# Attention batch 0 by query tiles, k in q's layout, zero products in gaps, and six x matrices turned by DMA

## Chip, core and metric

The kernel runs on one core of one Trainium2 chip. The metric is the device time of one execution in microseconds (us); the median of the runs shown is 271.3 us. One core has five engines that work from queues of their own: TensorE (PE in the profile, its weight loads PEld), VectorE (DVE), ScalarE (ACT), GpSimd (POOL) and SyncE (SP). SP here only issues DMAs; POOL issues some too and also computes.

## What is computed

For 8 batches and 12 heads, with 448 rows of 64 numbers: cosine attention, then a highway layer over the 3584 rows that the heads form together.

```python
q_n = q / (norm(q, axis=-1) + 1e-06);  k_n = k / (norm(k, axis=-1) + 1e-06)
scores = q_n @ k_n.T / tau                      # tau = 0.1
attn = softmax(scores);  x = attn @ v           # x: (8*448, 12*64) = (3584, 768)
H = relu(x @ w_h);  T = sigmoid(x @ w_t + b_t)
out = T * H + (1 - T) * x
```

The kernel leaves out the maximum of the softmax and the small constants, and makes the sigmoid from a tanh.

## The kernel before

**Work.** Heads are taken in pairs (p = 0..5 in a batch), and pairs in groups of two (g = 0..2). A batch goes through: loads (`ld_q` L293 on SP, `ld_k` L308 and `ld_v` L323 on POOL with a cast to fp16, tails of 64 rows `ld_kt`, `ld_vt` on SP); squares on ACT and sums on DVE (`norm_q`, `norm_k`, `norm_t`); an inverse root by seven small DVE steps (`newton`); scaling (`scale_q` L434, `scale_k` L495, `scale_kb` L502, nearly all on POOL); turning q and k with TensorE transposes and a DVE copy from PSUM (`turn_q` L446/L451, `turn_k` L460/L465/L471); `scores`; `attend`; and `ffn` for four row tiles.

**Layouts.** q is loaded so that a lane holds seven neighbouring rows (448 = 64 lanes x 7) of one head; two heads fill 128 lanes. The main part of k is 128 lanes x 3 rows of a head, and its last 64 rows come in a load of their own, are scaled apart (`kb`, zeros around them) and turned apart: eight transposes for a group, six of `kp` and two of `kb`.

**Attention** (`scores` L524, `attend` L548). For a pair: six products of 64x128 weights with 448 columns (L531) and one for both tails (L542), each followed by an exponential of 448 columns on ACT (L537, L544); then 3 x (1 + 6) products with 130 or 65 columns (L556, L561) and eight for the last 64 queries (L569); a reciprocal and a division on DVE (L576, L577) that write x. All 448 queries of a pair go at once, so x of a batch is complete only after its sixth pair.

**Highway layer** (`ffn` L583). A batch has three tiles of 128 rows and one that holds the last 64 twice, side by side. A tile's x is turned by six (three in the last tile) TensorE transposes (L600) and a DVE copy (L602); 24 products of 384 columns with w_t and w_h follow (L616; L613 in the last tile), then DVE and ACT work, sums on POOL (L642) and stores on SP (L649, L652).

**Order.** A `Plan` collects 1915 named operations in the program's order. `ORDER` is a list of their numbers, written out by hand or by a program elsewhere: every engine gets its operations in this order and works through them in it. `SLOTS` says which buffer of a ring each tile takes (`B` is the ring of the eight PSUM banks). Operations in `PORT` make a POOL operation wait for the DVE operation before it in `ORDER`. 18 products of zeros (`WARM`, L279) run at the start.

Of the kernel before, what the change touches and what calls it, by code (L numbers as in the profile page):

```python
# [93 lines left out]
""".split()  # L94
)

SLOTS = {
    "qr": "01010101",
    "kr": "0120120",
    "kt": "01010101",  # L100
    "kb": "01010101",
    "kp": "012345012345012345012345012345021435021435120534",
    "vr": "01010101",
    "vt": "01011010",
    "vp": "01010101",
# [96 lines left out]
def kernel(  # L202
# [11 lines left out]
    nc = tc.nc  # L214
# [555 lines left out]
```

## Time and profile before

| | us |
|---|---|
| runs: median (lowest to highest) of 3 | 271.3 (270.35 to 271.45) |
| the profiled execution | 270.06 |
| its span, first to last instruction | 268.3 |
| PE busy in the span | 251.6 (94%) |
| DVE busy | 233.4 (87%) |
| ACT busy | 214.5 (80%) |
| POOL busy | 169.8 (63%) |

The profile is of one execution. Matmuls are pipelined: one is shown from its start to its modelled end, so PE can look busy while it waits. The chain of waits goes back from the last instruction to whatever released each step, and gives every stretch of time to one engine or transfer. The granted clock is the share of TensorE's full clock that the chip gave it.

### The profile page before, as it was taken

Reading aid. Unit: us, or ns where it says so; the run is one execution under the profiler, and the core shown is the slowest. Engines: PE = TensorE matmul, PEld = TensorE weight load, DVE = VectorE, ACT = ScalarE, POOL = GpSimd, SP = SyncE. Lnnn points to the kernel's source line nnn. Section 1 sums busy time; section 2 is a strip of 40 time slices with the busy share of each in tenths; the row PEclk is TensorE's granted clock in tenths of the full one; section 3 lists DMA queues with packets and bytes.
Section 4 is the critical chain, followed back from the end, with each engine's and each line's share of the span. In section 5 each row is a group of like instructions: output and inputs, shape, how many; then the busy total and the mean of one; then the engine's idle time right before and its main releaser. Section 6 shows DMA issues by size and latency. Waiting matters only on the chain.

```text
span 268.3 us, 7687 instructions
## 1 busy us (share of the span) xinstructions
PE 251.6 (94%) x3042; PEld 158.8 (59%) x3042; DVE 233.4 (87%) x523; ACT 214.5 (80%) x421; POOL 169.8 (63%) x212
## 2 busy tenths in 40 slices
PE   8375999999999999999999999999999999999990
PEld 2122566656756576657656685666666675667660
DVE  2987988799999999999989899999998788657993
ACT  3389899999589997999899996999979757883120
POOL 6467878306975679668957397659555686320650
PEclk9755799999999999999999999999999999999998
DMA  7999999999307990496995972990513101052146
GB/s 173 298 290 181 208 270 261 213 255 126 44 18 221 234 182 14 146 257 159 151 142 185 164 107 67 330 135 4 147 23 100 29 15 49 0 147 65 29 135 190
DMA packets 51092, 38.64 MB, mean 144 GB/s; under 512 B 37488, under 2 KB 47856, under 8 KB 51056
## 3 DMA queue, kind: packets, MB, share of 16 engines
q1 hardware_dynamic: 25888, 26.75, 36.2%
q0 software_dynamic: 24896, 11.21, 33.1%
q8 instruction: 24, 0.39, 0.5%
q10 hardware_dynamic: 272, 0.20, 0.2%
q14 instruction: 12, 0.10, 0.1%
HBM read 38.34 MB, written 11.01 MB: 184 GB/s over the span
## 4 chain that ended last, share of the span: by engine, by line
PE 81%; DMA 6%; DVE 4%; ACT 4%; SPq 1%; issue 1%; POOL 1%; ACTq 0%; DVEq 0%
PE B L616 33%; PE B L531 12%; PE B L561 10%; PE B L613 5%; DMA os<-in_k_dram 4%; PE B L556 4%; PE B L600 4%; PE B L446 3%; PE B L542 3%; PE B L569 3%; PE B L460 3%; ACT E L537 3%; DMA out_dram<-os 1%; PE B L465 1%; DVE hm L628 1%
## 5 line engine op out<-in xcount | busy, mean ns | idle before, releaser
L537 ACT ACTIVATE E<-B 128x448 f16<-128x448 f32 x288 | 137.4, 577 | 15.6 <-PE B L531 12.6
L642 POOL TENSOR_TENSOR os<-x,hm 128x384 f32<-128x384 f16 x53 | 47.5, 911 | 50.2 <-DVE hm L637 39.6
L616 PEld LDWEIGHTS <-xT 128*128 128x128 f16 x576 | 51.2, 98 | 34.8 <-issue 7.5
L434 POOL TENSOR_TENSOR qn<-qr,y 128x448 f16<-128x448 f32 x47 | 43.4, 934 | 24.6 <-issue 8.1
L616 PE MATMUL B<-wh,xT 128*128 128x384 f16 x288 | 57.6, 326 | 0.0
L616 PE MATMUL B<-wt,xT 128*128 128x384 f16 x288 | 56.7, 326 | 0.0
L531 PE MATMUL B<-qT,kT 64*128 64x448 f16 x288 | 43.5, 367 | 2.8 <-DVE kT L473 1.5
L561 PE MATMUL B<-vp,E 128*128 128x65 f16 x864 | 44.5, 195 | 0.0
L561 PEld LDWEIGHTS <-E 128*128 128x128 f16 x864 | 39.1, 99 | 2.9
L632 ACT ACTIVATE tt<-z 128x768 f16<-128x768 f32 (+1 forms) x32 | 25.3, 793 | 18.5 <-DVE z L625 14.8
L495 POOL TENSOR_TENSOR kp<-kr,y 128x384 f16<-128x384 f16 x42 | 34.3, 827 | 8.2 <-DVE tt L634 2.6
L628 DVE SCALAR_TENSOR_TENSOR hm<-B,x 128x384 f16<-128x384 f32 x56 | 30.5, 549 | 3.0 <-PE B L616 1.7
L556 PE MATMUL B<-vp,Et 128*128 128x130 f16 x144 | 32.3, 224 | 0.0
L625 DVE TENSOR_TENSOR z<-B,bias 128x384 f32<-128x384 f32 x48 | 25.9, 551 | 6.5 <-PE B L616 5.5
L544 ACT ACTIVATE Et<-B 128x448 f16<-128x448 f32 x48 | 27.9, 597 | 3.1 <-PE B L542 2.8
L577 DVE SCALAR_TENSOR_TENSOR x<-B,rd 128x448 f16<-128x448 f32 x48 | 29.2, 617 | 0.6
L376 DVE TENSOR_REDUCE n<-sq 128x14 f32<-128x896 f32 (+1 forms) x25 | 25.8, 1040 | 1.2 <-ACT sq L368 1.2
L397 DVE TENSOR_REDUCE n<-sq 128x18 f32<-128x1152 f32 (+2 forms) x17 | 21.5, 1269 | 4.2 <-ACT sq L388 3.8
L368 ACT ACTIVATE sq<-qr 128x896 f32<-128x896 f32 (+1 forms) x24 | 23.1, 978 | 1.1 <-DMA qr<-in_q_dram 1.1
L531 PEld LDWEIGHTS <-kT 64*128 64x128 f16 x288 | 10.3, 94 | 20.1 <-issue 12.3
L556 PEld LDWEIGHTS <-Et 128*128 128x128 f16 x144 | 14.1, 98 | 7.9 <-issue 4.7
L542 PE MATMUL B<-qT,kT 128*128 128x448 f16 x48 | 17.4, 371 | 1.1 <-DVE kT L475 1.1
(59 smaller groups left out, 363.3 us busy)
## 6 DMA issues: line engine op xcount, KB each, us to landing
qr<-in_q_dram SPq DMA_DIRECT2D x7, 1344.0 KB, 7.6
out_dram<-os SPq DMA_DIRECT2D x48, 192.0 KB, 3.3
kr<-in_k_dram POOLq DMA_DIRECT2D x7, 576.0 KB, 12.2
vr<-in_v_dram POOLq DMA_DIRECT2D x7, 576.0 KB, 10.3
kt<-in_k_dram SPq DMA_DIRECT2D x16, 96.0 KB, 6.4
vt<-in_v_dram SPq DMA_DIRECT2D x16, 96.0 KB, 7.5
out_dram<-os SPq DMA_DIRECT2D x16, 96.0 KB, 2.9
qr<-in_q_dram SPq DMA_DIRECT2D x3, 448.0 KB, 6.9
```

The costliest lines, as they stand in the source:

```text
L434: ENG[eng].tensor_mul(R("qn", 3 * b + g)[:, :, t, :], R("qr", b)[:, g + 3 * t, :].rearrange("l (j d) -> l j d", d=D), R("y", b)[:, c : c + ...
L495: ENG[eng].tensor_mul(R("kp", 6 * b + p).rearrange("l c t d -> l t c d"), a, kcol(b, p))
L531: nc.tensor.matmul(R("B", ("S", n, c, t))[:, 0:S], lhsT=R("kT", i)[ln, s, 128 * c : 128 * c + 128], rhs=R("qT", i)[ln, s, :], start=True, ...
L537: nc.scalar.activation(R("E", n)[:, at : at + 7, :].rearrange("l j x -> l (j x)"), R("B", ("S", n, c, t))[:, 0:S], AF.Exp)
L544: op("ACT", f"expt {n}", lambda: nc.scalar.activation(R("Et", n).rearrange("l j x -> l (j x)"), R("B", ("St", n))[:, 0:S], AF.Exp), r=[("B ...
L556: nc.tensor.matmul(U[:, 2 * c : 2 * c + 2, :], lhsT=Et[:, 2 * c : 2 * c + 2, :].rearrange("l j x -> l (j x)"), rhs=vp[:, 6:8, 0:65], start ...
L561: nc.tensor.matmul(U[:, 2 * c + t, :], lhsT=E[:, at : at + 2, :].rearrange("l j x -> l (j x)"), rhs=vp[:, 3 * t + m, 0:65], start=False, s ...
L577: op("DVE", f"ev {n}", lambda: nc.vector.scalar_tensor_tensor(out=R("x", b)[:, :, D * p : D * p + D], in0=U_()[:, :, 0:D], scalar=0.0, in1 ...
L616: nc.tensor.matmul(P[:, 0:MH], lhsT=xT[:, cc, :], rhs=w_[:, cc, MH * mh : MH * mh + MH], start=(cc == 0), stop=(cc == CC - 1))
L625: op("DVE", f"za {g} {mh}", lambda at=at, sl=sl: nc.vector.tensor_add(R("z", g)[:, sl], R("B", at)[:, 0:MH], biast[:, :] if tail else bias ...
L628: op("DVE", f"hm {g} {mh}", lambda at=at, sl=sl, mh=mh: nc.vector.scalar_tensor_tensor(out=R("hm", g)[:, sl], in0=R("B", at)[:, 0:MH], sca ...
L642: op(eng, f"out {g} {mh}", lambda sl=sl, mh=mh: ENG[eng].tensor_add(R("os", g)[:, sl], xpart(mh), R("hm", g)[:, sl]), r=[("gg", g), ("x", ...
```

## The change

- **k like q.** k is loaded with q's layout (64 lanes x 7 rows, rows of 896 bytes after the cast), for batch 0 too, where before it came in fp32 on the SP and ACT queues. The tail's load, square, sum, scaling and zeros in `kb` go. `norm`, `scale` and `turn` serve q and k alike: a group of k has seven transposes, one copy of 2 x 384 columns and two small copies (`cpt`) of its last 64 rows; zeros around those are set once.
- **Inverse roots of batch 0** by two ACT operations (`lnexp`: exp(-0.5 ln)) for each group in place of seven DVE steps. ACT loads table set 6 first and set 0 after them (`table2`).
- **Batch 0 by query tiles** (`attend0`): for tile i of 128 queries (the last of 64), all three groups; x of tile i is complete when they are through, and `ffn(0, i)` reads that tile alone.
- **Zero products**: 37 more (`wf`), placed in `ORDER` among the first operations of PE.
- **x of batches 1 to 6** is turned by a transposing DMA on SP (`xd`, 24 of them: 18 of [128, 768] and 6 of [128, 384]), from x straight into xT. Batches 0 and 7 keep transposes and copies.
- **Rings**: kT and qT 3 to 4 buffers, xT 3 to 5.
- **Held loads**: a load of q or of v's tail for batch 1 or later waits for the ACT operation before it in `ORDER`.
- **ORDER and SLOTS** are new (1946 operations).

```diff
-PORT = ("nt", "gt", "gg", "vc", "qn", "kn", "kb", "vt", "out")
+PORT = ("nt", "gt", "gg", "vc", "qn", "kn", "vt", "out")
+        self.held = eng == "SP" and kind in ("ldq", "ldvt") and name.split()[1] != "0"
...
-    WARM = 18
+    WARM, NF = 18, 37
+    XDMA = range(1, B - 1)
+    LG = ((0, 0), (0, 28), (0, 56))
...
+    for i in range(NF):
+        op("PE", f"wf {i}", lambda i=i: nc.tensor.matmul(R("B", ("F", i))[:, :], lhsT=wz[:, 0:128], rhs=wz[:, 128:640],
+                                                         start=True, stop=True), r=[("wz",)], w=[("B", ("F", i))], mode="F")
...
+    def q_src(t, b):
+        return t[b].rearrange("(u s) (l j) d -> s l u (j d)", s=2, j=NJ)
+    def ld_qk(nm, b, gs=range(3)):
+        t, eng = (q, "SP") if nm == "q" else (k, "POOL")
...
+    def lnexp(b, lo, hi, parts):
+        i = (b, lo)
+        op("ACT", f"ln{hi - lo} {b} {lo}", lambda: nc.scalar.activation(
+            R("tu", i)[:, 0, lo:hi], R("n2", b)[:, lo:hi], AF.Ln, bias=eps[:, 0:1]),
...
+        op("ACT", f"ie{hi - lo} {b} {lo}", lambda: nc.scalar.activation(
+            R("y", b)[:, lo:hi], R("tu", i)[:, 0, lo:hi], AF.Exp, scale=-0.5),
...
+        if nm == "k":
+            for t in range(2):
+                ln = slice(64 * t, 64 * t + 64)
+                op("DVE", f"cpt {b} {g} {t}", lambda ln=ln, t=t: nc.vector.tensor_copy(
+                    turned("k", i)[ln, :, 384 + 64 * t : 448 + 64 * t], src()[ln, :, 384:448]),
...
+    def attend0(g, i):
+        q_, k_ = turned_of(g)
+        w = 128 if i < 3 else 64
...
+                    for c in range(NC):
+                        for t in range(2):
+                            ln, at = slice(64 * t, 64 * t + 64), unit(s)[0][t][c] - o - 512 * t
+                            nc.tensor.matmul(R("B", (A, B_)[t])[:, at : at + w], lhsT=k_()[ln, s, 128 * c : 128 * c + 128],
+                                             rhs=q_()[ln, s, 128 * i : 128 * i + w], start=True, stop=True)
...
+            for t, X, m in ((0, A, 512), (1, B_, 384)):
+                op("ACT", f"ex{m} {n}", lambda X=X, m=m, t=t, o=o: nc.scalar.activation(
+                    flat()[:, o + 512 * t : o + 512 * t + m], R("B", X)[:, 0:m], AF.Exp),
...
+        def turn_dma():
+            X = R("x", b)
+            nc.sync.dma_start(R("xT", g)[:, 0:nb, :], X[:, 6, :] if tail else X[:, 2 * i : 2 * i + 2, :].rearrange("l j m -> l (j m)"),
+                              transpose=True)
+        if b in XDMA:
+            op("SP", f"xd{nb} {g}", turn_dma, r=[xk], w=[("xT", g)])
+        else:
...
+                elif o.held:
+                    behind(made[0], act)
```

In the new order PE gets 41 zero products before its first transposes (`tk 0 0`, `tq 0 0`) and 14 in later gaps. The exponentials of query tiles 0 and 1 of all three groups stand ahead of most of tile 2's, and the first products of `ffn` follow them. An `xd` stands in SP's order soon after the last division of its batch; between that division and the first product that reads its xT, PE has other work:

| first tile of a batch | PE operations between |
|---|---|
| batch 1, tile 4 | 4 qk, 2 ff, 1 tk, 2 tq, 2 qkt |
| batch 2, tile 8 | 5 qk, 2 ff, 1 tk, 2 tq, 3 qkt, 3 av |
| batch 3, tile 12 | 4 qk, 2 ff, 2 tk, 2 tq, 2 qkt, 3 av |
| batch 4, tile 16 | 7 qk, 2 ff, 2 tk, 1 tq |
| batch 5, tile 21 | 3 qk, 4 ff, 2 fft, 1 tk, 2 tq |
| batch 6, tile 25 | 5 qk, 4 ff, 2 tk, 3 qkt, 6 av, 2 avt |

(qk is two products of 448 columns, qkt one, ff three of 384, fft six on half the columns, tk and tq seven transposes each, av 1 + 6 products, avt eight.)

More of the change, by code (lines that the diff above doesn't have):

```diff
@@ L121 @@
[L121 to L128 removed]
+    "qT": "01230123012301231023102",
@@ L144, in __init__ @@
         kind = name.split()[0].rstrip("0123456789")
-        self.port = eng in ("DVE", "POOL") and (kind in PORT or kind == "sqq")
+        self.held = eng == "SP" and kind in ("ldq", "ldvt") and name.split()[1] != "0"
+        self.port = eng in ("DVE", "POOL") and (kind in PORT or kind == "sq")
 class Plan:
@@ L220 @@
     NC, NJ = 3, 7
-    WARM = 18
+    WARM, NF = 18, 37
+    XDMA = range(1, B - 1)
+    GROUPS = ((0, 1), (1, 2), (2, 3)), ((0, 1), (1, 3)), ((0, 3),)
+    LG = ((0, 0), (0, 28), (0, 56))
+    SCALE = {("q", 0, 0): ("DVE", "POOL"), ("k", 0, 0): ("DVE", "POOL")}
     tau = float(tau)
@@ L273, with zf @@
                                     (t[0:64, :, 6, D : D + 1], 1.0), (t[64:128, :, 7, D : D + 1], 1.0)]), w=[("zvp",)])
-    for i, t in enumerate(TILES["kb"]):
-        op("DVE", f"zkb {i}", zero("DVE", [(t[0:64, :, 1, :], 0.0), (t[64:128, :, 0, :], 0.0)]), w=[("zkb",)])
-    op("DVE", "zw", zero("DVE", [(wz[:, :], 0.0)]), w=[("wz",)])
+    for i, t in enumerate(TILES["kT"]):
+        op("DVE", f"zkT {i}", zero("DVE", [(t[0:64, :, 448:512], 0.0), (t[64:128, :, 384:448], 0.0)]), w=[("zkT",)])
+    def zf():
+        t = turned("k", 0)
+        zero("DVE", [(t[0:64, :, 448:512], 0.0), (t[64:128, :, 384:448], 0.0)])()
+    op("DVE", "zkf", zf, w=[("x", "f", "z")])
+    op("DVE", "zw", zero("DVE", [(wz[:, :], 0.0), (eps[:, :], 1e-14)]), w=[("wz",), ("eps",)])
     for i in range(WARM):
@@ L344, in ld_b, with col @@
         op("SP", "ldb", fn, w=[("b",)])
[L347 to L366 removed]
+    def col(nm, g):
+        return 28 * g + 14 * (nm == "k")
@@ new lines, with norm, fn @@
+    SQV = ()
+    SPLIT = {("q", 0, 0): ("ACT", "DVE"), ("k", 0, 0): ("ACT", "ACT")}
+    def norm(nm, b, g):
+        i = (nm, b, g)
+        sc = tau if nm == "q" else 1.0
+        engs = SPLIT.get(i, (("DVE" if i in SQV else "ACT"),))
+        n = 3 - len(engs)
+        for t, eng in enumerate(engs):
+            ts = slice(t, t + n)
+            def fn(eng=eng, ts=ts):
+                src = R(nm + "r", b)[:, g::3, :][:, ts]
+                dst = R("sq", i).rearrange("l (t x) -> l t x", t=2)[:, ts]
@@ L400, in norm_t @@
[L400 to L406 removed]
+                    nc.vector.scalar_tensor_tensor(out=dst, in0=src, scalar=sc * sc, in1=src, op0=ALU.mult, op1=ALU.mult)
@@ L445, in fn @@
             for j in range(NJ):
-                nc.tensor.transpose(T[:, j], R("qn", i)[:, j].rearrange("l t d -> l (t d)"), ident[:, :])
-        op("PE", f"tq {b} {g}", fn, r=[("qn", i, 0), ("qn", i, 1), ("id",)], w=[("B", ("Tq", i))], mode="F")
+                to = j if nm == "q" or j == 6 else 2 * (j % 3) + j // 3
+                nc.tensor.transpose(T[:, to], R(nm + "n", i)[:, j].rearrange("l t d -> l (t d)"), ident[:, :])
+        op("PE", f"t{nm} {b} {g}", fn, r=[(nm + "n", i, 0), (nm + "n", i, 1), ("id",)] + ([("wm",)] if i == 0 and nm == "k" else []),
+           w=[("B", at)], mode="F")
@@ L448, in turn_q, with src @@
+        def src():
+            return R16(at)[:, 0:896].rearrange("p (s x) -> p s x", s=2)
         for s in range(2) if parts == 2 else (None,):
             def cp(s=s):
-                a = slice(0, 896) if s is None else slice(448 * s, 448 * s + 448)
-                nc.vector.tensor_copy(R("qT", i).rearrange("p s x -> p (s x)")[:, a], R16(("Tq", i))[:, a])
-            op("DVE", f"cpq{parts} {b} {g} {s}", cp, r=[("B", ("Tq", i))], w=[("qT", i, s)] if s is not None else [("qT", i, 0), ("qT", i, 1)])
@@ L498, in scale_kb @@
-    def scale_kb(b, eng):
-        for ab in range(2):
-            def fn(ab=ab):
-                ln, c = slice(64 * ab, 64 * ab + 64), KCS[b > 0][1]
-                ENG[eng].tensor_mul(R("kb", b)[ln, :, ab, :], R("kt", b)[ln, :, :],
-                                    R("y", b)[ln, c : c + 6].unsqueeze(2).to_broadcast([64, NP, D]))
-            op(eng, f"kb {b} {ab}", fn, r=[("kt", b), ("zkb",), ("y", b, "t")], w=[("kb", b)])
+                ss, d = slice(0, 2) if s is None else slice(s, s + 1), turned(nm, i)
@@ L583, in ffn, with turned_of @@
+    def turned_of(g):
+        return lambda: turned("q", g), lambda: turned("k", g)
     def ffn(b, i):
         g = 4 * b + i
+        xk = ("x", b) if b else ("x", b, i)
         tail = i == 3
@@ L700 @@
-        scale_kb(b, "POOL")
-        if b == 0:
-            copy_v(b, 0, 3)
-            copy_v(b, 3, 6)
-        else:
-            copy_v(b, 0, 6)
+            if b == 0:
+                ld_w(moe_w_t, wt, "wt")
+                ld_w(moe_w_h, wh, "wh")
+                ld_b()
+        else:
+            ld_qk("q", b)
+            ld_qk("k", b)
+            ld_v(b)
+            ld_vt(b)
+        for g in range(NG):
+            for nm in "qk":
+                norm(nm, b, g)
+        for g0, g1 in GROUPS[min(b, 2)]:
+            (lnexp if (b, 28 * g0) in LG else newton)(b, 28 * g0, 28 * g1, [(nm, g) for g in range(g0, g1) for nm in "qk"])
@@ L706 @@
+        for p0 in (0, 3) if b == 0 else (0,):
+            copy_v(b, p0, p0 + (3 if b == 0 else 6))
         cast_vt(b, "POOL")
         for g in range(NG):
-            first = b == 0 and g == 0
-            scale_q(b, g, ("DVE", "POOL") if first else ("POOL", "POOL"))
-            for s in range(2):
-                scale_k(b, 2 * g + s, "DVE" if first else "POOL")
-            turn_q(b, g, 2 if first else 1)
-            turn_k(b, g)
-        for p in range(NP):
-            scores(b, p)
-            attend(b, p)
+            for nm in "qk":
+                scale(nm, b, g, SCALE.get((nm, b, g), ("POOL", "POOL")))
+                turn(nm, b, g, 1)
@@ L717, with behind @@
+        if b == 0:
+            for i in range(4):
+                for g in range(NG):
+                    attend0(g, i)
+        else:
+            for p in range(NP):
+                scores(b, p)
+                attend(b, p)
         for i in range(4):
             ffn(b, i)
+    def behind(a, b):
+        tc.add_manual_dep(a, b.name, mybir.DependencyInfo(mybir.DependencyClass.Sync, mybir.DependencyReason.SCHED_ONLY),
+                          reason="order")
     with nc.allow_low_precision(reason="fp16 operands of the products and gates as given"):
@@ L721 @@
         with tc.manual_schedule():
-            before = None
+            before = act = None
             for o in pl.ordered(ORDER, SLOTS):
@@ L725 @@
                 o.fn()
-                if o.port:
-                    made = [i for i in nc.cur_bb.bb.instructions[made:] if i.engine == ENG[o.eng].engine]
-                    if o.eng == "DVE":
-                        before = made[-1]
-                    elif before is not None:
-                        tc.add_manual_dep(made[0], before.name, mybir.DependencyInfo(
-                            mybir.DependencyClass.Sync, mybir.DependencyReason.SCHED_ONLY), reason="port")
-                        before = None
+                made = [i for i in nc.cur_bb.bb.instructions[made:] if i.engine == ENG[o.eng].engine]
+                if o.eng == "ACT":
+                    act = made[-1]
+                elif o.held:
+                    behind(made[0], act)
+                elif o.port and o.eng == "DVE":
+                    before = made[-1]
+                elif o.port and before is not None:
+                    behind(made[0], before)
+                    before = None
 _INS = ['q', 'k', 'v', 'tau', 'moe_w_h', 'moe_w_t', 'moe_b_t']
```

354 lines of the change are left out of this document (150 added, 204 removed), and 148 rows, old and new, of the table ORDER.

## The prediction

> **What bounds the kernel now.** I read the page first: the span, the shares of the engines, and the slices of a fortieth.
>
> ```profile
> span 268.3 us, 7687 instructions
> PE 251.6 (94%) x3042; PEld 158.8 (59%) x3042; DVE 233.4 (87%) x523; ACT 214.5 (80%) x421; POOL 169.8 (63%) x212
> PE   8375999999999999999999999999999999999990
> PEclk9755799999999999999999999999999999999998
> ```
>
> PE is full from the fifth slice on, and VectorE (87%) and ScalarE (80%) are close behind it. Ahead of that stand four slices (27 us) in which PE is half idle and the granted clock is at 0.5 to 0.7. So there are two questions: what PE has to do in the long middle, and what keeps it from starting. The chain of waits answers the first (44 to 200 us), the busy time by stretches both.
>
> ```profile
> by line: PE B L616 41.5%; PE B L531 14.5%; PE B L561 10.9%; PE B L613 6.5%; PE B L600 4.5%; PE B L556 4.4%; PE B L446 4.4%; PE B L542 4.2%; PE B L569 3.8%; PE B L460 3.6%; PE B L465 1.1%; DVE xT L602 0.3%; DVE hm L628 0.3%; issue 0.1%
> ...
> 10.00:28.00 18.00, 11.26 (x54) 4.45 (x54) 15.31 (x45) 14.25 (x27) 14.18 (x18) 0.50 1.30 241
> 28.00:44.00 16.00, 15.70 (x247) 10.65 (x246) 13.14 (x38) 14.91 (x33) 12.03 (x15) 0.92 1.15 252
> 44.00:200.00 156.00, 155.87 (x1972) 100.69 (x1971) 148.00 (x309) 142.90 (x279) 108.14 (x129) 1.00 0.76 147
> ```
>
> In the middle 99.3% of the chain is PE: a product taken out there shortens the run by its own time, unless VectorE (148.0 of 156, 95%) takes over. From 28 to 44 us PE looks busy, but the chain says otherwise:
>
> ```profile
> by line: ACT E L537 16.1%; PE B L561 13.3%; ACT Et L544 11.0%; DVE x L577 10.6%; issue 9.2%; PE B L531 7.7%; PE B L556 6.6%; PE B L460 5.8%; PE B L569 5.3%; DVE qT L451 3.9%; DVE kT L471 3.8%; DVE rd L576 3.3%; PE B L446 3.1%; PE B L465 0.7
> L616 PE MATMUL B<-wt,xT x288: 322/326/337, 45.8 to 257.7; 128*128 128x384 f16 x144
> ```
>
> Its PE shares sum to 42.5%: for some 9 of 16 us PE follows exponentials, divisions and copies. The products that could fill it, the gate's, begin at 45.8 us, since batch 0's x is complete only then.
>
> **Part 1: PE's own work.** x is turned 21 transposes a batch; six batches leave PE: 126. k takes seven transposes for a group and not eight: 24 fewer. The chain has a row of 18:
>
> ```profile
> 71.42 1.00 PE B L600 x18
> 72.87 1.46 PE B L616 x9
> 74.34 0.68 PE B L531 x6
> ```
>
> 1.00/18 is 55.6 ns: 126 of them 7.0 us, 24 of them 1.3 us. Batch 0's scores are cut finer: 144 small products (108 of 128 columns, 36 of 64) and 24 tails for 36 and 6 of 448. Two 64-row products run side by side (0.68/6 is 113 ns each, 227 a pair), so the old ones cost 18 x 0.227 and six tails of at most that, some 5.4 us. If pairs stay pairs and 128 columns cost a transpose's 56 ns, the new cost about 5 us; if each goes alone, 168 x 0.056 = 9.4, 4.1 more. I take no difference, since the pairs of L531 are the nearest row.
>
> **Part 2: the start.** The steps up to the first exponential of now, then the loads:
>
> ```profile
> 1.27 6.75 PE L279 MATMUL B<-wz 128*128 128x512 f16 x18 [1.27 <-DVE wz L266]
> 6.78 0.74 PEld L279 LDWEIGHTS <-wz 128*128 128x128 f16 x4 [0.26 <-issue]
> 12.11 0.91 PE L446 MATMUL B<-ident,qn 128*128 128x128 f16 x7 [4.09 <-DVE tu L421]
> 14.58 1.44 ACT L388 ACTIVATE sq<-os 128x384 f32<-128x384 f32 x2 [2.82 <-DVE kp L495]
> 16.77 4.43 ACT L537 ACTIVATE E<-B 128x448 f16<-128x448 f32 x10
> ...
> L368 ACT ACTIVATE sq<-qr 128x448 f32<-128x448 f32 x1 | 0.6, 560 | 0.0
> L368 ACT ACTIVATE sq<-qr 128x896 f32<-128x896 f32 x23 | 22.5, 996 | 1.1 <-DMA qr<-in_q_dram 1.1
> L376 DVE TENSOR_REDUCE n<-sq 128x7 f32<-128x448 f32 x2 | 1.1, 610 | 0.0
> L434 POOL TENSOR_TENSOR qn<-qr,y 128x448 f16<-128x448 f32 x47 | 43.4, 934 | 24.6 <-issue 8.1
> ...
> qr<-in_q_dram SPq DMA_DIRECT2D x3, 448.0 KB, 6.9
> wt<-in_moe_w_t_dram POOLq DMA_DIRECT2D x1, 1152.0 KB, 20.3
> ```
>
> In the new kernel group 0 of q and k come at once: 6.9 us, on two queues, so at about 7. Three half squares on ACT (0.56 each), a last sum of 0.61, two small ACT steps and two scalings of 0.93 on POOL end near 11.7. PE meanwhile has 41 zero products in front: 18 took until 8.0, and the last four weight loads stand 0.2 apart, so 23 more end at 12.9. That is the later: 14 transposes at 56 ns until 13.7, copies and first products until an estimated 15.4, 1.4 us before the first exponential of now. Without the queue of zero products it would be 14.2.
>
> From there 24 exponentials (ten took 4.43 us, so 10.6) and three squares of 0.98 finish the first two query tiles: 28.9; with products, division, turn and copy the gate can start at about 30, against 45.8. w_t takes 20.3 from issue to landing and must be issued by 9.7 to be there; behind batch 0's loads on POOL I assume so. From 30 to 44 us PE then has gate products for the stretches in which the chain is off PE: at most 9 us. ACT, at 14.91 of 16, still feeds the rest, so I take 40%, 3.6 us. For the clock, at 0.50 from 10 to 28 us now and perhaps whole when the 55 zero products keep PE busy, I count nothing more, since ACT and not PE leads there. Start: 1.4 + 3.6 = **5.0 us**, between 0 (the chain stays on ACT) and 2.6 + 9 = 11.6.
>
> **Part 3: the cover.** The rows behind the edits that I cost at nothing:
>
> ```profile
> L602 DVE COPY xT<-B 128x768 f16<-128x768 f16 x24 | 12.8, 549 | 0.7 <-PE B L600 0.7
> L602 DVE COPY xT<-B 128x384 f16<-128x384 f16 x8 | 2.8, 349 | 0.2 <-PE B L600 0.2
> L404 DVE TENSOR_REDUCE n<-sq 128x6 f32<-128x384 f32 x8 | 4.4, 545 | 0.0
> L397 DVE TENSOR_REDUCE n<-sq 128x18 f32<-128x1152 f32 x15 | 20.0, 1339 | 0.3 <-ACT sq L391 0.3
> L376 DVE TENSOR_REDUCE n<-sq 128x14 f32<-128x896 f32 x23 | 24.7, 1077 | 1.2 <-ACT sq L368 1.2
> L471 DVE COPY kT<-B 128x1024 f16<-128x1024 f16 x21 | 14.3, 681 | 0.7 <-PE B L465 0.7
> L475 DVE COPY kT<-B 128x256 f16<-128x256 f16 x3 | 0.8, 283 | 0.0
> ```
>
> VectorE, in a batch of 1 to 6: minus 3 x 0.549 + 0.349 = 2.0 (x copies), minus 0.55 (tail sums), plus 3 x 1.077 - 2 x 1.339 = 0.55 (k's sums), minus 3 x (0.681 - 0.549) = 0.4 (k copies), plus six `cpt` of at most 0.283 each, some 1.3: 1.1 us less in a batch, beside 1.3 us less on PE (21 + 3 transposes). Both loads fall together, so 95% stays 95% and PE's gain stands; if VectorE sets the pace, 6 x 0.2 = 1.2 us of it are lost. The exponentials are 42 as before with as many elements. POOL's k scaling is now L434's; POOL is on no stretch of the chain above.
>
> **Part 4: the transposing DMAs.** No DMA of this kernel transposes, and none goes from SBUF to SBUF. The nearest rows:
>
> ```profile
> out_dram<-os SPq DMA_DIRECT2D x48, 192.0 KB, 3.3
> out_dram<-os SPq DMA_DIRECT2D x16, 96.0 KB, 2.9
> qr<-in_q_dram SPq DMA_DIRECT2D x7, 1344.0 KB, 7.6
> kr<-in_k_dram POOLq DMA_DIRECT2D x7, 576.0 KB, 12.2
> ```
>
> A tile of x in fp16 is 128 x 768 x 2 bytes: 192 KB, exactly a store's size, from the same queue. I take its 3.3 us; the ends are 2.9 and 12.2. PE waits in order, so what counts is PE's work between a batch's last division and the first product of its first tile. The order gives the operations, and starts in the timeline of PE the rest of their times:
>
> ```profile
> 40.25 0.36 PE L542 MATMUL B<-qT,kT 128*128 128x448 f16 x1
> 40.45 0.22 PE L556 MATMUL B<-vp,Et 128*128 128x130 f16 x1
> ...
> 42.09 0.22 PE L556 MATMUL B<-vp,Et 128*128 128x130 f16 x1
> ...
> 42.34 0.22 PE L556 MATMUL B<-vp,Et 128*128 128x130 f16 x1
> ```
>
> qkt takes 0.20 from its start to the next, av 0.25 (I give avt the same), qk 0.23, ff and fft 0.49 (three times 1.46/9), tk and tq 0.39. Tile 4: 4 x 0.23 + 2 x 0.49 + 3 x 0.39 + 2 x 0.20 = 3.5; likewise tiles 8, 12, 16, 21 and 25: 4.6, 4.6, 3.8, 4.8, 6.5. Together 27.8. At 3.3 none stalls; other tiles have more room. Behind an `xd` that waits for x stand SP's stores and held loads; the ring of four `os` buffers covers the first.
>
> [...]
>
> **The sum.** Against the profiled span: 268.3 - 7.0 - 1.3 - 5.0 = 255.0. The execution was 270.06, 1.8 over its span: 256.8. The runs' median of 271.3 stands 1.2 over that execution: **258.0 us**. The end stays, since batch 7 keeps its transposes and its order of sums and stores.
>
> **Rivals.** (A) *The transposing DMAs land late* and PE stands at each batch's first tile. With a landing L the stalls are 6L - 27.8; they eat the whole gain of 13.3 at L = 6.9. At 7.6, what a q load takes on this queue, they are 17.8: 276. At 12.2 they are 45.4: 303. For it: the transfers share DMA engines with loads (0.76 of their time in the middle), and the held loads stand among them on SP. Against it: stores of the same size land in 3.3 under the same load. (B) *The start gains nothing*: zero products delay the first transposes, ACT (14.25 of 18, 14.91 of 16) sets the pace, or w_h, issued only after batch 1's first k scalings, comes late: 263. (C) *The middle gives it back*: more and smaller copies for k on a VectorE at 95%, and POOL's rule to wait for VectorE, cost the 8.3 us that PE saves: 266. (D) *The change doesn't do what it says*: neither the gate starts earlier nor does PE's shorter work show, since another engine sets both: 271.
>
> **How the numbers follow.** Forecast 0.52 (its own range 250 to 262), A 0.19, B 0.13, C 0.09, D 0.07. The low end, 250, is the start's bound (6.6 more than taken) and 1.4 for the spread of runs; the high end takes in D and reaches to where A begins, 273, since A alone is left out. About 0.5% (1.4 us) is what a measurement of this kernel tells from no change. Faster by more: forecast, B and C, 0.74; within: D, 0.07; slower: A, 0.19.
>
> **What would show it.** First gate product (L616's successor) near 30 us; PEclk at 0.9 or more in slices two to five; transposes on PE 126 + 24 fewer; `xd` landings near 3.3 us and PE waiting for xT under 0.5 us a batch; DVE and ACT shares up to some 88% and 85% with shorter spans. The prediction is wrong if xT's wait shows on PE at each batch's first tile, if the first exponential comes after 17 us, or if the middle's chain turns to VectorE or ScalarE.

## The result and the profile after

The changed kernel takes **275.0 us** (274.3 to 275.4, four runs) against 270.8 for the kernel before beside it: a ratio of 1.016 (95% interval 1.012 to 1.019). It is slower by 1.6%; forecast were 258.0 and a range of 250 to 273. The profiled execution took 275.44.

The page of the changed kernel, its span, shares and slices:

```profile
span 273.7 us, 7737 instructions
PE 251.3 (92%) x3055; PEld 155.4 (57%) x3055; DVE 225.0 (82%) x530; ACT 217.5 (79%) x425; POOL 165.7 (61%) x205
PE   8947997799999999976999999999999999999991
PEclk9995999999999999997999999999999999999997
```

Two dents are new in PE's row (a slice is 6.8 us): 41 to 55 us and 116 to 130 us. The clock's row reads 9 in the first three slices and 5 in the fourth, where the kernel before has 9, 7, 5, 5, 7 (first five slices). Busy time by stretches (PE, PEld, DVE, ACT, POOL, then clock, DMA share, GB/s), and one stretch of the kernel before for comparison:

```profile
10.00:28.00 18.00, 12.15 (x120) 6.93 (x119) 11.77 (x22) 12.24 (x24) 8.74 (x11) 0.81 1.13 199
28.00:44.00 16.00, 15.15 (x268) 11.24 (x265) 13.09 (x38) 15.60 (x32) 8.18 (x10) 1.00 0.55 119
44.00:200.00 156.00, 147.64 (x1870) 91.76 (x1870) 140.83 (x327) 141.85 (x278) 108.31 (x128) 0.99 0.86 168
60.00:80.00 20.00, 19.40 (x278) 12.28 (x274) 19.66 (x43) 19.83 (x38) 14.66 (x18) 1.00 1.03 223
```

```profile
60.00:80.00 20.00, 20.00 (x258) 13.31 (x257) 19.35 (x42) 15.88 (x29) 16.02 (x19) 1.00 0.49 66
```

From 44 to 200 us PE is busy for 147.64 us where it was 155.87, and from 60 to 80 us ScalarE has no room left (19.83 of 20, before 15.88).

Busy time hides short waits between pipelined products, so I use a second measure below, PE's **lost time**: the time t less the products that have started by then, each at what it takes in rows of the kernel before at a clock of 1.00 (1.46/9, so 162 ns, for 384 columns, 1.00/18, so 56, for 128, and so on). All products together come to 220.0 us before and 212.1 after; products of zeros are not counted. So 7.9 us of work did leave PE. The losses ate it (each row is one execution; "stores reordered" is run 12 below, "four repairs" run 17):

| PE's lost time by | 44 us | 60 | 80 | 100 | 120 | 140 | 200 | 253 |
|---|---|---|---|---|---|---|---|---|
| before | 28.6 | 30.1 | 31.1 | 32.5 | 34.1 | 35.2 | 39.3 | 41.8 |
| changed | 28.2 | 32.7 | 37.0 | 39.2 | 40.9 | 47.2 | 51.9 | 55.3 |
| changed, stores reordered | 29.4 | 31.9 | 36.8 | 38.3 | 40.9 | 42.1 | 46.6 | 49.3 |
| changed, four repairs | 25.1 | 27.7 | 31.8 | 33.5 | 35.4 | 36.9 | 41.6 | 43.7 |

The second and the third row have the same operations in the same order at the start and still differ by 1.2 us at 44 us, so a difference of that size between two rows tells nothing. Three places stand out in the second row: nothing is gained by 44 us, 8.8 us go between 44 and 80 (before: 2.5), and 6.3 between 120 and 140 (before: 1.1).

**The stall at 121 us.** First what the SP queue waited for in 85 to 130 us (total, times, longest), then its issues there, then POOL, DVE and PE by the timeline:

```profile
SPq L648 <- DVE x L530: 28.4, 2, 15.9
```

```profile
90.18 18.41 SPq L648 DMA_TRANSPOSE xT<-x  x2
108.69 0.53 SPq L327 DMA_DIRECT2D qr<-in_q_dram  x1
109.31 6.32 SPq L648 DMA_TRANSPOSE xT<-x  x3
115.69 1.88 SPq L704 DMA_DIRECT2D out_dram<-os  x2
```

```profile
123.05 1.77 POOL L694 TENSOR_TENSOR os<-x,hm 128x384 f32<-128x384 f16 x2 [3.89 <-DMA out_dram<-os]
```

```profile
124.86 0.56 DVE L680 SCALAR_TENSOR_TENSOR hm<-B,x 128x384 f16<-128x384 f32 x1 [4.08 <-POOL os L694]
```

```profile
125.47 0.22 PE L509 MATMUL B<-vp,Et 128*128 128x130 f16 x1 [3.72 <-DVE hm L680]
```

Read it from the bottom. PE waits for a PSUM bank that DVE's `hm` frees; DVE waits for POOL, which must free `hm`; POOL waits for an `os` buffer, which a store frees. That store (tile 5) had its sums ready at 105.87, but on SP it stands behind a transposing DMA that waited 15.9 us for batch 2's x, then behind a q load of 1344 KB and three more transposing DMAs. It is issued at 115.69, and POOL has its buffer at 123.05. The ring of four is shorter still than that: the stores of tiles 1 and 2, whose sums POOL had finished by 90.6, stand even further back on SP and are issued from 124.47 on, so two more buffers are held all that time.

**The start**, by the timelines of ACT, PE and POOL:

```profile
18.05 0.95 ACT L377 ACTIVATE sq<-qr 128x896 f32<-128x896 f32 x1 [4.28 <-DMA qr<-in_q_dram]
18.91 0.30 ACT L411 ACTIVATE tu<-n,eps 128x28 f32<-128x28 f32 x1
19.24 0.23 ACT L414 ACTIVATE y<-tu 128x28 f32<-128x28 f32 x1
19.49 1.28 ACT L287 ACT_TABLE_LOAD   x1
20.78 0.49 ACT L574 ACTIVATE E<-B 128x384 f16<-128x384 f32 x1
```

```profile
14.30 0.56 PE L439 MATMUL B<-ident,kn 128*128 128x128 f16 x7 [1.21 <-POOL kn L424]
36.40 0.51 PE L644 MATMUL B<-ident,x 128*128 128x128 f16 x6
...
52.41 0.51 PE L644 MATMUL B<-ident,x 128*128 128x128 f16 x6
57.19 0.33 PE L644 MATMUL B<-ident,x 128*128 128x128 f16 x3
```

```profile
23.36 0.50 POOL L472 CAST vp<-vt 64x384 f16<-64x384 f32 x1 [1.98 <-DMA vt<-in_v_dram]
26.93 0.51 POOL L472 CAST vp<-vt 64x384 f16<-64x384 f32 x1 [3.07 <-DMA vt<-in_v_dram]
```

The first exponential comes at 20.78, 4.0 us later than before: ahead of it ACT has a square of *batch 1's* q, whose load it awaits for 4.28 us, and behind that the last inverse root and the second table load. POOL then waits 5.05 us in all for batch 0's v tail. On SP that tail stands behind two loads of batch 1's q, and these are held loads: the first of them waits for a square on ACT.

```profile
SPq L329 <- ACT sq L377: 7.5, 1, 7.5
```

And batch 0's x is complete tile by tile as meant, the first two tiles at 36.8 us by DVE's last division; but the third comes at 48.2 and the fourth at 56.3. Before, all four came at 43.7.

### The profile page after: what moved, and what is told of

Read it like the earlier page. It is cut to its first block, busy times and chain, and to the rows that moved or that the text cites. A ratio compares the mean times of both kernels' runs of the same rounds, so it can differ in the third digit from the quotient of the medians.

```text
span 273.7 us, 7737 instructions
## 1 busy us (share of the span) xinstructions
PE 251.3 (92%) x3055; PEld 155.4 (57%) x3055; DVE 225.0 (82%) x530; ACT 217.5 (79%) x425; POOL 165.7 (61%) x205
## 3 DMA queue, kind: packets, MB, share of 16 engines
q0 software_dynamic: 20416, 12.58, 32.7%
## 5 line engine op out<-in xcount | busy, mean ns | idle before, releaser
L490 ACT ACTIVATE E<-B 128x448 f16<-128x448 f32 x252 | 119.8, 573 | 13.8 <-PE B L484 12.6
L424 POOL TENSOR_TENSOR kn<-kr,y 128x448 f16<-128x448 f16 x47 | 43.9, 944 | 21.5 <-PE B L561 5.8
L385 DVE TENSOR_REDUCE n<-sq 128x14 f32<-128x896 f32 (+1 forms) x50 | 51.1, 1036 | 5.1 <-ACT sq L377 5.0
L514 PE MATMUL B<-vp,E 128*128 128x65 f16 x756 | 38.2, 194 | 0.2 <-ACT E L490 0.2
L684 ACT ACTIVATE tt<-z 128x768 f16<-128x768 f32 (+1 forms) x32 | 25.3, 796 | 15.9 <-DVE z L677 15.9
L514 PEld LDWEIGHTS <-E 128*128 128x128 f16 x756 | 33.6, 98 | 6.9 <-issue 3.9
L484 PE MATMUL B<-qT,kT 64*128 64x448 f16 x252 | 36.1, 354 | 0.4 <-DVE qT L449 0.3
L377 ACT ACTIVATE sq<-kr 128x896 f32<-128x896 f16 (+1 forms) x25 | 23.3, 955 | 2.7 <-DMA kr<-in_k_dram 2.7
L574 ACT ACTIVATE E<-B 128x384 f16<-128x384 f32 (+1 forms) x42 | 20.1, 560 | 1.7 <-PE B L561 0.7
L449 DVE COPY qT<-B 128x896 f16<-128x896 f16 x23 | 14.1, 615 | 6.6 <-PE B L439 4.7
L439 PE MATMUL B<-ident,kn 128*128 128x128 f16 x168 | 14.1, 227 | 4.6 <-ACT E L574 3.3
## 6 DMA issues: line engine op xcount, KB each, us to landing
wt<-in_moe_w_t_dram POOLq DMA_DIRECT2D x1, 1152.0 KB, 19.4
```

Of the source, the lines that this page charges most:

```text
L377: nc.scalar.activation(dst, src, AF.Square, scale=sc)
L385: nc.vector.reduce_sum(R("n2", b)[:, c : c + 7 * n], a, axis=AX.X)
L424: ENG[eng].tensor_mul(R(nm + "n", i)[:, :, t, :], R(nm + "r", b)[:, g + 3 * t, :].rearrange("l (j d) -> l j d", d=D), R("y", b)[:, c : c + ...
L484: nc.tensor.matmul(R("B", ("S", n, c, t))[:, 0:S], lhsT=R("kT", i)[ln, s, 128 * c : 128 * c + 128], rhs=R("qT", i)[ln, s, :], start=True, ...
L490: nc.scalar.activation(R("E", n)[:, at : at + 7, :].rearrange("l j x -> l (j x)"), R("B", ("S", n, c, t))[:, 0:S], AF.Exp)
L514: nc.tensor.matmul(U[:, 2 * c + t, :], lhsT=E[:, at : at + 2, :].rearrange("l j x -> l (j x)"), rhs=vp[:, 3 * t + m, 0:65], start=False, s ...
```

## The experiments

Orders are shown by the names of operations. "Faster" and "slower" are against the kernel before; where an edit is priced, it is by the difference of two ratios, times 270 us. Intervals of 95% are in brackets; a difference carries those of both ratios, 1.2 to 1.9 us either way.

**1. The first exponential.**

```diff
-ACT: sq2 q 1 0 0 ahead of ln 0 56, ie 0 56, table2
+ACT: sq2 q 1 0 0 behind ex512 0 1 1;  sq2 q 1 1 0 behind ex512 0 0 0
```

> The changed kernel (275.0 us) with the squares of batch 1's q (groups 0 and 1) moved behind the first exponentials of batch 0 on ScalarE, and their sums behind them on VectorE. Theory W (waits that the new order made): in the changed kernel the first exponential starts at 20.78 us, since ScalarE waits 4.28 us for batch 1's q, then does that square, ln, exp and the table load of 1.28; without the wait it starts near 17.0, and the lag of 4 us that ScalarE carries into 60 to 80 us goes: 271 to 272 us. Rival P (pace: VectorE and ScalarE, 91 to 95% busy from 44 to 120 us, set the time whatever PE waits for): the first exponential comes earlier, the time stays within 1 us of 275.

Measured: 275.9, ratio 1.022 [1.019, 1.025]. The first exponential came at 17.78, and the time did not fall. In this run POOL waited 7.0 us for the v tail in place of 5.05: another wait stood right behind the one removed.

**2. Every store right behind its sums.**

```diff
-SP: ... xd6 8, ldq 5 0, xd6 9, xd6 10, xd3 11, st 5 ...
+SP: each st g behind its last sum in ORDER
```

> The changed kernel with each store placed right behind its two sums in the order of operations, so that no transposing DMA and no held q load stands between them on SP. Theory W: store 5, ready at 105.9 us, left at 115.7 and landed some 7 us later, and POOL's next sum, VectorE and PE (3.97 us lost at 121.4) waited for its buffer; the same at 158.5 us in smaller. With the stores in front PE's loss between 110 and 130 us falls by 4 us and the time to about 270.5. Rival P: the stall moves to another wait of the same length, since VectorE and POOL are the pace: 274 to 275.

Measured: 282.8, ratio 1.048 [1.045, 1.050]. The stall at 121 us went, but now the transposing DMAs stand behind stores that wait. PE's waits (total, times, longest):

```profile
PE B L667 <- DMA xT<-x: 8.8, 3, 6.3
PE B L438 <- ACT E L573: 2.5, 1, 2.5
```

**3. No zero products in the gaps.** `NF = 0` in place of 37.

> The changed kernel without its 37 added zero products. Theory W: PE's first transposes wait for POOL's scaling (1.21 us idle ahead of them at 14.30), not for zero products, which end at 12.9; so they cost nothing, and what they give is the clock (0.81 from 10 to 28 us, 1.00 from 28 to 44, against 0.50 and 0.92 before the change). Since ScalarE leads there, the time without them is 0 to 1 us longer: 275 to 276. Rival F (the zero products delay the start, as I feared in the prediction): 1 to 2 us shorter, 273 to 274. A third reading, that the cold clock reaches the chain: 277 or more.

Measured: 278.0, ratio 1.028 [1.024, 1.032], 3.3 us more than the changed kernel. The granted clock falls from 0.81 to 0.59 between 10 and 28 us:

```profile
10.00:28.00 18.00, 8.93 (x97) 6.78 (x98) 11.88 (x21) 12.26 (x24) 9.03 (x11) 0.59 1.13 199
```

But the time is not lost there. By 44 us PE has lost as much as in the changed kernel (within 0.2 us), and by 120 us 0.6 less. The profiled execution, 1.9 us longer than the changed kernel's, falls behind between 120 and 200 us, first at the stall, where PE's wait for `hm` is 5.1 us in place of 3.72:

```profile
PE B L506 <- DVE hm L677: 5.1, 1, 5.1
```

So the clock is not shown to be the cause of the 3.3 us. What is stays open.

**4. x turned by PE again.** `XDMA = ()`, with transposes and copies put into the order behind the places of the DMAs.

> The changed kernel with x of batches 1 to 6 turned by TensorE and copied by VectorE again, each pair placed between the transposing DMA's place and the first product that reads its xT. Theory W: PE gets 126 transposes (7.0 us) and VectorE 12 us of copies back, but SP has no transposing DMA that waits ahead of stores, so the 4 us stall near 121 us goes: 275 to 279. Rival L (the transposing DMAs themselves cost more than they save, by landing late or by slowing other transfers): faster than 273. Rival P: 12 us more for VectorE shows in full, 283 or more.

Measured: 300.8, ratio 1.111 [1.107, 1.115]. The order was not made for them: PE waited 14 us in all on their copies. The run prices a poor order, not the DMAs.

**5 and 12. The stores in the order in which they are ready** (by the sums' and x's times in the trace, so that none stands behind a DMA that waits), with w_h's load earlier and without.

```diff
-SP: st 0, st 3, xd3 7, xd6 8, ldq 5 0, xd6 9, xd6 10, xd3 11, st 5, ldvt 5, st 7, ldvt 4, st 1, st 2
+SP: st 1, ldq 4 0, xd6 6, st 3, xd3 7, st 2, st 5, xd6 8, ldq 5 0, xd6 9, xd6 10, xd3 11, st 7, ldvt 5, st 4
-POOL: ldwh behind kn 1 0 1                 (5 only)
+POOL: ldwh behind vt 0 1
```

> The changed kernel with two repairs: w_h's load is issued on POOL behind the last cast of batch 0's v tail, ahead of batch 1's scalings; and each store of batches 0 to 5 stands on SP in the order of the times at which its sums and the transposing DMAs' x were ready in the changed kernel's trace, so that none stands behind an xd that waits. Theory W (waits that the new order made: w_h 2.8 us, store behind xd 5.2 us): both gaps of PE go, 275.0 - 8.0 = 267, at most 270. Theory P (VectorE and ScalarE, 98% busy from 60 to 120 us, set the pace): the gaps go, but the middle refills, 272 to 275. If stores are late again elsewhere as with each store right behind its sums: over 275.

> The changed kernel with the stores in the order in which they are ready, and w_h's load where the changed kernel has it. If the stores behind waiting DMAs were the whole of what both repairs gained, and w_h's wait costs nothing in the end (as the earlier first exponential gained nothing): 269.6, as with both. If w_h's wait of 2.8 us counts: 272.

Measured: 269.6, ratio 0.997 [0.995, 1.000], with both; 269.5, 0.998 [0.996, 1.001], with the stores alone. The stores' places cost 4.7 us, all of them together: the stall at 121 us went, and the edit moves stores 1 and 2 as well as store 5, so it does not tell which of them the ring lacked. The wait of PE for w_h, 2.8 us at 49.6 in the changed kernel, is not told apart, since it was 0.2 in run 12 too: loading w_h earlier is worth 0.3 us by these two ratios, which is within their noise.

**6 and 9. VectorE, then ScalarE, with less to do.**

```diff
-nc.vector.reduce_sum(n2, a)
+nc.vector.reduce_sum(n2, a[:, :, 0:32])
-nc.scalar.activation(dst, src, AF.Square)                              (9 only)
+nc.scalar.activation(dst[..., 0:32], src[..., 0:32], AF.Square)
```

> The changed kernel, in which VectorE sums the squares of q and k over 32 of their 64 elements (the squares are doubled, so the inverse roots are of another sum: half of the squares is left out). VectorE has some 0.5 us less for each of 48 sums, 3 us a batch, about 12% of its work; nothing else changes. Theory P: the stretch from 60 to 120 us, in which PE falls 5 to 6 us behind, recovers, and the time falls by 4 us or more, to 271 or less. Theory W: VectorE's room is worth little, since PE waits there for what stands late in the order: within 1.5 us of 275.0.

> The changed kernel with both repairs (w_h early, stores in the order in which they are ready: 269.6), in which ScalarE squares 32 of 64 elements of q and k of batches 1 to 7 and VectorE sums those 32 (half of the squares is left out). ScalarE has some 0.45 us less for each of 42 squares (19 us of 217), VectorE 0.5 us less for each sum (21 us). Theory S (what PE saved is lost since ScalarE, 97 to 99% busy from 44 to 120 us, sets the pace of the products with q and k): PE's lost time from 44 to 253 us falls from 19.5 to some 12, the time to 262 or 263. Theory W (only single waits cost): within 1.5 us of 269.6.

Measured: 274.2, ratio 1.014 [1.010, 1.018]: VectorE's room alone is worth nothing measurable. With ScalarE lightened too, on the repaired kernel: 266.6, 0.989 [0.985, 0.993], 2.3 us less than run 5; neither 1.5 nor 7. By 253 us PE had lost 47.5 where run 5 lost 49.1. From 60 to 80 us ScalarE had more room (18.03 of 20 busy), and PE hardly gained:

```profile
60.00:80.00 20.00, 19.48 (x273) 12.26 (x270) 17.68 (x47) 18.03 (x39) 15.16 (x18) 1.00 1.11 241
```

**7, 10 and 13. The transposing DMAs alone, in the order before**: 16 of 24 tiles, 78 transposes; with the squares halved, without and with them.

```diff
+if g in (5, 6, 7, 10, 11, 13, 14, 15, 17, 18, 19, 22, 23, 24, 26, 27):
+    op("SP", f"xd{nb} {g}", turn_dma, r=[("x", b)], w=[("xT", g)])
-xT=(3, [128, CC, 128], FP16)
+xT=(4, [128, CC, 128], FP16)
```

> The kernel before, with its order, in which 16 of the 24 tiles of x of batches 1 to 6 (10 of 768 columns, 6 of 384: those with 5 us and more of PE's work between x and their products) are turned by a transposing DMA on SP, at the place where x is ready or 7.5 us of PE's work ahead of their products; xT has four buffers in place of three. 78 transposes leave PE (4.3 us) and 7.6 us of copies leave VectorE. Theory W (PE's own work is what the middle costs, the DMAs themselves are harmless): 270.2 - 4.3 = 266. Theory L (the DMAs or what stands behind them on SP cost as much as they save): 270 or above.

> The control of the run beside it: the kernel before with half of the squares and sums of q and of k's main part left out in batches 1 to 7 (k's sums are also taken in another order of rows). ScalarE has some 10 us less in q's squares and as much in k's, VectorE 20. The chain from 44 to 200 us is PE for 99.3%, so the theory that PE alone sets the middle of the kernel before expects no more than 1 us: 269 to 270. Theory S in a strong form (ScalarE holds PE back in this kernel too): 267 or less.

> The kernel before with 16 tiles of x turned by DMA (269.1), and in it half of the squares and sums of q and of k's main part left out in batches 1 to 7, as in the control (268.8 without the DMAs). 78 transposes, 4.3 us of PE, are away in both. Theory S (PE's saving shows only as far as ScalarE and VectorE follow): with both lightened by some 20 us the saving shows, 264.5 to 266. Theory L (the transposing DMAs, or what stands behind them on SP, cost what the transposes saved): their price stays, 267.5 to 268.5.

Measured: 269.1, ratio 0.996 [0.994, 0.998] for the DMAs; 268.8, 0.998 [0.995, 1.000] for the control; 267.8, 0.990 [0.987, 0.993] for both. So 4.3 us of matmul work shorten the run by 1.1, and by 2.1 where VectorE and ScalarE have room. But the difference of 1.0 between the two carries the intervals of three ratios, 1.2 us either way, and 267.8 lies where theory L expected it (267.5 to 268.5), not theory S (264.5 to 266). So it is not shown that the other two engines eat the saving. The DMAs landed in 2.9 us (median) and PE waited for none of them, which leaves of theory L what stands behind them on SP. Where the rest of the 4.3 us went is open; the loss grows in small steps all along the run. The longest waits that the trace names from 44 us on in run 7, where the kernel before has none, come to 1.3 us:

```profile
PE B L623 <- DVE xT L609: 0.6, 1, 0.6
PE B L460 <- POOL kp L495: 0.4, 1, 0.4
PE B L465 <- POOL kb L502: 0.3, 1, 0.3
```

**8 and 11. Zero products in the kernel before**, 22 in its gaps up to 24 us; then with the DMAs of run 7.

```diff
+for i in range(22):
+    op("PE", f"wf {i}", ...)     # 12 ahead of tq 0 0, 4, 3 and 3 in the next gaps
```

> The kernel before with 22 more zero products: 12 behind the 18, ahead of the first transposes, and 4, 3 and 3 in PE's gaps of 15 to 24 us; nothing else. If the clock of the first stretch is what they buy (leaving out 37 cost the changed kernel 3 us): the granted clock from 10 to 44 us rises and the time falls by 1 to 3 us, to 267 to 269. If ScalarE leads the first 28 us whatever the clock: 270 to 271.

> The kernel before with both edits that were each worth 1 us alone: 16 tiles of x turned by DMA (269.1) and 22 more zero products (269.0). If they add: 268.0. If the DMAs' gain is eaten by ScalarE's pace, an earlier start doesn't help it: 268.5 to 269.

Measured: 269.0, ratio 0.996 [0.993, 0.998]; together 268.7, 0.995 [0.992, 0.999]. The clock from 10 to 28 us is the changed kernel's, 0.81 where it was 0.50, and the zero products are worth 1.1 us here; in the profile PE is 1.2 us ahead by 44 us and stays so:

```profile
10.00:28.00 18.00, 13.75 (x91) 5.86 (x92) 15.50 (x44) 14.35 (x27) 14.23 (x18) 0.81 1.30 242
```

The two edits together bring 1.2 us. The sum of their prices, 2.2, lies at the edge of the interval, so whether they add is not told.

**14, 17 and 19. The start again**: run 5 with run 1's edit; then with the v tail's load moved too; then that move by itself, on the changed kernel.

```diff
-SP: ldq 0 2, ldq 1 0, ldq 1 1, ldvt 0
+SP: ldq 0 2, ldvt 0, ldq 1 0, ldq 1 1      (17 and 19)
```

> The changed kernel with w_h early, the stores in the order in which they are ready, and the squares of batch 1's q behind batch 0's first exponentials, so that the first exponential comes 3 us earlier. If the first exponential's wait is hidden by what the middle can take (as it was with the store's wait still there): 269 to 270. If it was only masked by that wait: 267.

> The changed kernel with w_h early, the stores in the order in which they are ready, the first exponential earlier, and batch 0's v tail loaded right behind its q, ahead of batch 1's q (in the earlier runs it was issued at 11 us behind batch 1's loads, landed 13 us later, and POOL's casts of it waited 7.0 us, with all of batch 0's attention behind them). Theory B0 (the start is held by batch 0's v tail, which stands behind batch 1's loads and beside w_t's): PE loses 2 to 4 us less by 44 us, and the time falls to 266 to 268. If the start is masked by the middle, as with the first exponential: 269 to 271.

> The changed kernel with one edit: batch 0's v tail is loaded right behind its q. If the v tail was the start's limit by itself: POOL's casts no longer wait, PE loses 2 to 3 us less by 44 us, and with the stores' wait of 5.4 us still there the time is 271 to 273. If it was only the limit once the first exponential, w_h and the stores were mended: 274 to 276.

Measured: 270.8, ratio 1.001 [0.998, 1.004], without the move; **264.0, ratio 0.978 [0.972, 0.984], with it**; 272.2, 1.006 [1.003, 1.010], the move alone. So the v tail's place costs 6.2 us once the other three are mended, and 2.6 in the changed kernel as it stands. In the changed kernel the tail is issued at 11.15 us behind batch 1's held q loads, beside k of batch 1 and w_t, and takes 13.5 us; moved, it is cast by POOL at 19.42 without a wait (last line, run 17):

```profile
wt<-in_moe_w_t_dram POOLq DMA_DIRECT2D x1, 1152.0 KB, 19.4
kr<-in_k_dram POOLq DMA_DIRECT2D x1, 672.0 KB, 13.8
vt<-in_v_dram SPq DMA_DIRECT2D x2, 96.0 KB, 13.5
```

```profile
19.42 1.06 POOL L471 CAST vp<-vt 64x384 f16<-64x384 f32 x2
```

The stretches of run 17:

```profile
10.00:28.00 18.00, 14.04 (x172) 8.46 (x171) 13.64 (x28) 14.92 (x30) 10.81 (x13) 0.91 1.24 225
28.00:44.00 16.00, 15.57 (x255) 10.82 (x251) 14.11 (x45) 15.96 (x34) 7.30 (x9) 1.00 1.00 180
60.00:80.00 20.00, 19.18 (x228) 11.28 (x227) 19.74 (x46) 20.00 (x40) 12.39 (x15) 1.00 0.94 159
```

ACT does 30.9 us of work between 10 and 44 us where the changed kernel has 27.8. The granted clock over the same stretch is 0.95, where run 14 and the changed kernel had 0.90. This kernel is faster than the kernel before and than the changed one.

**15 and 18. Batch 1 prepared earlier**, its squares, inverse roots and scalings moved among batch 0's exponentials: on run 14, and on run 17 with the third q load placed later.

```diff
-ACT: ... ex512 2 2 0 ... sq2 k 1 2 0, sq2 k 1 1 0 ... sq2 q 1 2 0
+ACT: sq2 k 1 0 0, sq2 k 1 1 0, ... ex512 2 0 1, sq2 k 1 2 0, ex384 2 0 0, sq2 q 1 2 0
-SP: ldq 1 2 behind batch 0's exponentials
+SP: ldq 1 2 behind ldvt 0  (15);  behind ex512 1 1 0  (18)
```

> The changed kernel with w_h early, the stores in the order in which they are ready, the first exponential earlier, and batch 1 prepared earlier: its third q group is loaded behind batch 0's v tail, the squares and sums of its second and third groups stand among batch 0's exponentials of the third group of heads, and the inverse roots and scalings follow at once. Theory B1 (the order by query tiles puts batch 1 off: its last group is turned at 62 us against 52 before, and PE lacks its products from 44 to 80 us): PE loses 2 to 4 us less there, and the time falls to 266 to 268. If ScalarE alone sets this stretch, the same squares only stand elsewhere in it: 269 to 271.

> The same with batch 1 prepared earlier as in the last run, but its third q group loaded only behind the first exponentials of the second group of heads, so that it doesn't delay the v tail (there PE waited 5.0 us for it). Theory B1 (batch 1's late preparation is what PE lacks from 44 to 80 us): 2 us or more below the run beside it. If ScalarE alone sets that stretch: the same as the run beside it, within 1 us.

Measured: 277.7, ratio 1.032 [1.026, 1.037], and 273.0, 1.010 [1.005, 1.016], 8.7 us above run 17. In run 15, with the q load right behind the v tail, PE waited 5.0 us for that tail's cast. In run 18 that wait is gone, and PE has still lost 7.7 us more than in run 17 by 44 us, ACT standing 9.6 us for PE's scores in batch 0. The granted clock, as a mean of the profiled execution, was 0.967, where run 17 has 0.99; what part of the loss that is, is not shown. What holds PE there first I have not settled. Preparing batch 1 at batch 0's cost is no remedy in this form.

## Why the prediction was wrong, point by point

- **Part 1 held.** 7.9 us of work left PE, 8.3 were forecast; the pairs of batch 0's small products stayed pairs (27 ns a product from 28 to 44 us, at a granted clock of 1.00).
- **"A product taken out there shortens the run by its own time, unless VectorE (148.0 of 156, 95%) takes over" failed.** Taken out by themselves, 4.3 us gave 1.1. A chain that is all PE says which wait ended last, not how far behind the second one is. Where the missing 3.2 us went is not shown: lightening the other two engines (in run 7 VectorE is busy for 93% and ScalarE for 92% of 44 to 200 us) brings 1.0 with an uncertainty of 1.2, and the trace names waits of 1.3.
- **Part 2 failed in its first step.** I named what stands ahead of the first exponential by the program's dependencies, and not by what the queues hold in the new order: batch 1's square on ACT, the v tail's cast on POOL, and on SP the held loads ahead of that tail. The first came at 20.78 and not 15.4 (17.78 without the square; the rest fits the two scalings on POOL, which ended at 14.24 and not 11.7); the gate began at 37.62 and not 30. By 44 us PE has gained 0.4 us where 5.0 were forecast. Of the two only the v tail is a limit that pays (6.2 us, or 2.6 alone); the first exponential by itself is worth nothing. w_t was there in time, as assumed (issued at 8.91 and 19.4 to land). The zero products did not delay the transposes, which waited 1.21 us for POOL's scaling of k. And the clock, counted at nothing, is a term of 1.1 us in the kernel before (run 8, 0.81 from 10 to 28 us where it was 0.50); in the changed kernel no run prices it.
- **Part 3**: VectorE's load fell as said (233.4 to 225.0) and its room is worth nothing measurable (run 6). ScalarE, of which the part says only that its exponentials stay as they were, fills up between 60 and 80 us, though from 44 to 200 us it has no more to do than before (141.85, before 142.90): its work comes later.
- **Part 4: the price of the DMAs was right, the queue was wrong.** Issue, waiters and landing of all 24:

```profile
L648 SPq DMA_TRANSPOSE xT<-x x24: 1202/1245/3287, 78.1 to 232.2; - x24
...
  PEld L668: 1.1, 2
  PE B L668: 0.3, 1
...
DMA to landing us min/median/max: 2.6/3.1/8.6
```

They land in a median of 3.1 us (3.3 taken), and PE waits 0.3 us for them in the whole run (its weight loads 1.1). SP spends 1.24 us (median of 18) on the issue of one of 192 KB, and 1.20 to 1.62 us on each of the six of 96 KB. The landing is counted from the start of the issue, so that time is part of the 3.1 us and not on top of it. What failed is the half sentence "the ring of four os buffers covers the first". I named what is queued behind a waiting `xd` and did not work out for how long: the wait was 15.9 us, four more DMAs stood between it and the store, two more buffers were held by stores 1 and 2, and the ring was short for 3.9 us. With the stores in another order the time is 4.7 us shorter.
- **Rival A** gave 276 and the time was 275, but that is luck: PE hardly waited for its landings (0.3 us). **Rival B** named w_h, which no run shows to cost anything, and zero products, which helped. No rival had the stores or the v tail.
- **The sum**: with the queues mended (run 17) the change gives 264.0 where 258.0 were forecast. Against the kernel before beside it that is 5.9 us less, where 13.3 were forecast. Of the 7.4 that are missing, 4.2 are the stretch from 44 to 80 us, where PE loses 6.7 and the kernel before 2.5, with ScalarE at 20.00 of 20 from 60 to 80; 1.5 are the start, where 3.5 of the 5.0 came; the rest is spread over the run. That ScalarE is the cause from 44 to 80 us is not shown: with it lightened in run 9, PE lost 6.0 there and not 7.2. It stays open.

## What to carry to other kernels

SP worked through its queue in the order written: a store whose sums were ready at 105.87 us left at 115.69, behind a DMA that waited 15.9 us. So when a step is moved onto a queue, work out for each of its waits how long it will last and what stands behind it for that long, down to the buffer that runs out. The late store and the late v tail are the same mistake on the same queue: a ready DMA behind one that waits (15.9 us for x, 7.5 for a square on ACT). At a start, follow every input of the first stage through the queue of the engine that must touch it; here the small load that came behind the next batch's big ones was the one that was late. And a chain that is all one engine is no proof that its work is worth its own time: here, with two other engines 92% and 93% busy, 4.3 us taken off the one that led gave 1.1.

## What the runs showed of the hardware that was not expected

- A 192 KB transposing DMA from SBUF to SBUF holds SP's queue for 1.24 us (median of 18 in the changed kernel), and one of 96 KB for no less (1.20 to 1.62, six of them); the issue of a store's half takes about 0.6. The 24 land in a median of 3.1 us, a store of 192 KB in 3.0.
- Two loads of 96 KB, issued at 11.15 us, took 13.5 us to land beside 672 KB and 1152 KB of the POOL queue; the median of all 16 such loads of the changed kernel is 4.3. In run 17, where they are loaded ahead of batch 1's q, POOL casts them at 19.42 without a wait, and the move is worth 6.2 us in the repaired kernel (run 17 beside run 14).
- With zero products in PE's gaps the granted clock from 10 to 28 us is 0.81 (the changed kernel, run 8); it is 0.50 without them in the kernel before and 0.59 in the changed one (run 3). In the kernel before 22 of them are worth 1.1 us; the changed kernel is 3.3 us longer without its 37, but loses that time behind 120 us, not at the start.
